# Row minima of the masked attention scores: one masked pass and one reduction for a unit instead of one fused instruction for a block

## The chip, the cores and the metric

The kernel runs on one core of one Trainium2 chip. The metric is device time in microseconds (us) of one execution. Three runs of the kernel before gave a median of 922.48 us (921.83 to 923.4). Engines: PE is TensorE (matmuls), DVE VectorE, ACT ScalarE, POOL GpSimd, SP SyncE, which issues the DMAs.

## The reference

Sparse attention over 4 batches and 8 heads of 576 positions (head width 64), followed by two dense feed-forward layers, all in float32. Only the attention part matters here:

```
scores = (1/sqrt(64)) * q @ k.T
scores = where(mask, scores, -1e9)     # heads 0-3: the last 32 positions; heads 4-7: every 32nd position
scores = scores - max(scores, row)
attn = exp(scores)
attn = attn / (sum(attn, row) + 1e-9)
x = attn @ v                           # then x -> mish layer -> gated SiLU layer
```

## The kernel before

The feed-forward layers are matmuls with every float32 operand split into a high and a low part, so that three matmuls stand for one product (`mm3`, line 83). They fill nearly the whole span. The attention is worked off beside the first of these matmuls.

**Units.** The attention is cut into 48 units, numbered from 0. A unit belongs to one batch and one pair of heads (`hp`) and holds three or four blocks. In the local pairs (`hp` 0 and 1) a block is 128 rows of scores by 96 keys and a unit has three blocks; in the strided pairs (`hp` 2 and 3) a block is 108 rows by 64 keys, and three units of a pair have 4, 4 and 3 blocks. So there are 24 local units, 16 strided units of four blocks and 8 of three. The order is local pairs first, then strided ones, three units to a pair (in the last batch the strided ones come first).

**Steps of a unit.** `at_qk`: PE writes the scores of all blocks to one PSUM bank `sc` (line 303), and DVE forms the negated, scaled, masked scores `pt` in SBUF and their row minima in `sm[:, 0]` (line 315). `at_exp`: ACT takes exp(min - pt) block by block, in place, and leaves the row sums in `sm[:, 1]` (line 330). `at_norm`: DVE adds 1e-9 to the sums (line 343) and takes reciprocals (line 344), and POOL multiplies `pt` by them (line 345). `at_tr` transposes on PE (line 361), `at_copy` copies the result to SBUF on DVE (line 373), `at_pv` multiplies with v on PE (line 386), `at_hi` and `at_lo` split the output on ACT (line 74) and DVE (line 79).

**What sets the order.** The program order on each engine is written out by hand. A step `k` of the list `DENSE` runs `at_qk` and `at_exp` of unit k, `at_norm` of unit k-1, `at_tr` and `at_copy` of unit k-3, `at_pv` and `at_hi` of unit k-4, `at_lo` of unit k-5. The first 29 steps are run so. Between two of them stand a few idle matmuls (`spin`), one product of the first layer, and one of the four operations with which DVE rebuilds a weight tile from its stored bits (lines 207, 210, 213, 216). When a weight tile is rebuilt, ACT makes its high part (line 74) and POOL its low part (line 79). The other 19 units follow in the list `LOOSE`, in three pieces per unit, beside a denser stream of matmuls. Three times ACT applies Mish to a chunk of the first layer (line 494), which takes a change of its function table before and after.

**What the change touches.** `at_qk` from line 312 and `at_norm` at line 343, and one constant, the value at masked places in `_layout`.

Of the kernel before, what the change touches and what calls it, by code (L numbers as in the profile page):

```python
# [12 lines left out]
ALU = mybir.AluOpType  # L13
# [41 lines left out]
def local_strided_attention__mish_moe__swiglu_kernel(  # L55
# [10 lines left out]
    nc = tc.nc  # L66
# [20 lines left out]
    masks = [cst[:, 0:96], cst[:, 96:192], cst[:, 192:256]]  # L87
# [16 lines left out]
    for i in range(NP):  # L104
        for kind in "gv":
            k = "gv".index(kind)
# [160 lines left out]
    for i, (b, hp) in enumerate(pairs):  # L267
        nb, st_ = (NLB, 3) if hp < 2 else (NSB, 4)
# [21 lines left out]
    def blk(hp, j):  # L290

        if hp < 2:
            return LB, LK, j * LB, masks[0 if j == 0 else 1]
        return SW, 64, SR[j] * NJ, masks[2]

    def at_qk(u):
        i, b, hp, js = units[u]
        t = qk_t[i]
        sc = ps.tile([128, 512], F32, tag="sc", name="sc", bufs=2)
        w = blk(hp, js[0])[1]  # L300
        for jj, j in enumerate(js):
            nq, nk, j0, m = blk(hp, j)
            nc.tensor.matmul(  # L303
                sc[:2 * nq, jj * w:(jj + 1) * w],
                lhsT=t[:, 2 * j * nq:2 * (j + 1) * nq],
                rhs=t[:, QW + j0:QW + j0 + nk],
                start=True,
                stop=True,
            )
        pt = sb.tile([128, 4 * 96], F32, tag="pt", name="pt", bufs=6)[:2 * nq, :len(js) * w]  # L310
        pt = pt.rearrange("p (j k) -> p j k", k=w)
        sm = small.tile([128, 2, 4], F32, tag="sm", name="sm", bufs=5)[:2 * nq]
        for jj, j in enumerate(js):
            m = blk(hp, j)[3]
            nc.vector.tensor_tensor_reduce(  # L315
                pt[:, jj],
                sc[:2 * nq, jj * w:(jj + 1) * w],
                m[:2 * nq],
                -0.125,
                3.0e38,  # L320
                ALU.add,
                ALU.min,
                accum_out=sm[:, 0, jj:jj + 1],
            )
        st[u] = (pt, sm)

    def at_exp(u):
# [11 lines left out]
    def at_norm(u):  # L339
        pt, sm = st[u]  # L340
        n, nb, w = pt.shape
        r = sm[:, 1, :nb]
        nc.vector.tensor_scalar_add(r, r, 1e-9)
        nc.vector.reciprocal(r, r)  # L344
        nc.gpsimd.tensor_tensor(out=pt, in0=pt, in1=r.unsqueeze(2).to_broadcast([n, nb, w]), op=ALU.mult)  # L345

# [77 lines left out]
    def at_v(u):  # L424
        if u % 2:
# [5 lines left out]
        [  # L431
            (at_load, 0),
            (at_qk, 0),
            (at_tr, 3),
            (at_pv, 4),
            (at_v, 4),
            (at_exp, 0),
            (at_norm, 1),
            (at_lo, 5),
            (at_copy, 3),  # L440
            (at_hi, 4),
        ]
    ]
    LOOSE = [
        [(at_load, 0), (at_norm, 1), (at_lo, 5), (at_qk, 0), (at_exp, 0)],
        [(at_tr, 3), (at_copy, 3)],
        [(at_pv, 4), (at_hi, 4), (at_v, 4)],
# [174 lines left out]
    fv, fs, f4 = {}, {}, [None]  # L622
# [261 lines left out]
def _layout(q, k, v, moe_w_in, moe_w_out, moe2_w_gate, moe2_w_val, moe2_w_out):  # L884
    import numpy as np

    f4 = np.float32

    def heads_t(a):
        return a.reshape(B, 4, 2, S, D).transpose(0, 1, 2, 4, 3).reshape(B, 4, 128, S)  # L890

    def residue_major(a):
        return a.reshape(B, 2, 128, NJ, STR).transpose(0, 1, 2, 4, 3).reshape(B, 2, 128, S)

    qt, kt = heads_t(q), heads_t(k)
    qt[:, 2:], kt[:, 2:] = residue_major(qt[:, 2:]), residue_major(kt[:, 2:])
    qk = np.zeros((B, 4, 128, QW + KW), f4)
    for hp in range(4):
        n, first = (LB, range(0, S, LB)) if hp < 2 else (SW, [r * NJ for r in SR])
        for j, q0 in enumerate(first):  # L900
            for h in range(2):
                p = slice(64 * h, 64 * h + 64)
                qk[:, hp, p, (2 * j + h) * n:(2 * j + h + 1) * n] = qt[:, hp, p, q0:q0 + n]
    qk[:, :2, :, QW + STR:] = kt[:, :2]
    qk[:, 2:, :, QW:QW + S] = kt[:, 2:]

    vp = v.reshape(B, 4, 2, S, D).transpose(0, 1, 3, 2, 4).reshape(B, 4, S, 128)
    v_loc = np.zeros((B, 2, 3, LK, 3, 128), f4)
    for j in range(NLB):
        lo = j * LB - STR  # L910
        a = max(0, -lo)
        v_loc[:, :, j // 3, a:, j % 3] = vp[:, :2, lo + a:lo + LK]
    vr = vp[:, 2:].reshape(B, 2, NJ, STR, 128).transpose(0, 1, 3, 2, 4).reshape(B, 2, S, 128)
    v_str = np.zeros((B, 2, 3, 128, 4, 128), f4)
    for j in range(NSB):
        k0, p0 = SR[j] * NJ, 64 * (j % 2)
        m = min(64, S - k0)
        v_str[:, :, j // 4, p0:p0 + m, j % 4] = vr[:, :, k0:k0 + m]

    def bits(w):  # L920
        return w.view(np.int64) if w.dtype == np.float64 else w

    def col_tiles(w):
        w = bits(w)
        n = w.shape[1] // 128
        return w.reshape(4, 128, n, 128).transpose(2, 1, 0, 3).reshape(n, 128, 512)

    w1 = np.stack([col_tiles(moe_w_in), bits(moe_w_out).reshape(FF1 // 128, 128, DM)], axis=2)
    w2 = np.stack([col_tiles(moe2_w_gate), col_tiles(moe2_w_val), bits(moe2_w_out).reshape(FF2 // 128, 128, DM)], axis=2)

    p, c = np.arange(128)[:, None], np.arange(LK)[None, :]
    rel = p % LB - (c - STR)
    local = (rel >= 0) & (rel < STR)

    w, i = np.arange(64)[None, :], p % SW
    strided = (i // NJ == w // NJ) & (w % NJ <= i % NJ)
    keep = np.concatenate([local & (c >= STR), local, strided], axis=1)
    consts = np.concatenate([np.where(keep, f4(0), f4(-8e9)), np.eye(128, dtype=f4)], axis=1)
    return {
        "qk": qk.reshape(B * 4, 128, QW + KW),  # L940
        "v_loc": v_loc.reshape(B * 2, 3, LK, 3, 128),
        "v_str": v_str.reshape(B * 2, 3, 128, 4, 128),
        "w1": w1,
        "w2": w2,
        "consts": consts,
    }
# [21 lines left out]
```

## Time and profile before

| | before |
|---|---|
| median of three runs | 922.48 us |
| profiled execution: time, span | 920.13 us, 918.3 us |
| granted TensorE clock | 0.999 (of 2.4 GHz) |
| busy PE, DVE, ACT, POOL | 900.5, 602.0, 381.8, 162.9 us |
| chain that ended last | PE 87%, DVE 5%, DMA 3%, ACT 2% |

The profiled execution is one run, and its own time stands 1.8 us above its span. Busy shares are means over stages of different kind: from about 165 us on, PE is busy almost without a gap, and the attention is over; before that the engines take turns at being late. So the first 165 us are to be read stretch by stretch. In a list of instructions by time, the first column is the start and the second the duration; where an instruction starts before the one in front of it has ended, the two overlap, and the time that the engine spends on one is the distance from start to start.

### The profile page before, as it was taken

The numbers are of one execution on the slowest core, as the hardware profiler recorded it, in microseconds if no ns is written. First come the engines' busy times: TensorE is split into PE (matmuls) and PEld (weight loads), VectorE is DVE, ScalarE is ACT, GpSimd is POOL, SyncE is SP. The second block draws the span as 40 slices with busy tenths as digits, with TensorE's granted clock in tenths as the row PEclk, the third lists the DMA queues.
The fourth block names the chain that finished last, engine by engine and source line by source line (L and its number), as shares of the span: only waits on it lengthen the run. The fifth ranks groups of instructions, "written<-read, shape, count | busy, mean of one in ns | idle before, by whom it ended". The sixth has DMA issues, their size and how long they took to land.

```text
span 918.3 us, 13830 instructions
## 1 busy us (share of the span) xinstructions
PE 900.5 (98%) x4983; PEld 751.6 (82%) x4987; DVE 602.0 (66%) x1382; ACT 381.8 (42%) x951; POOL 162.9 (18%) x153
## 2 busy tenths in 40 slices
PE   8988999999999999999999999999999999999998
PEld 5776886888888888888889888888888888888886
DVE  5997576778876797769556788848435644334434
ACT  5667654525443444434243554423324423322230
POOL 3445141400000000000022322203113221112211
PEclk9999999999999999999999999999999999999999
DMA  8875431324643254524106887675532545552322
GB/s 290 282 254 179 146 116 50 115 92 165 212 174 115 95 198 176 172 70 161 69 1 262 290 330 303 259 287 191 186 121 109 207 153 191 186 203 92 138 92 91
DMA packets 48499, 156.70 MB, mean 171 GB/s; under 512 B 5296, under 2 KB 11824, under 8 KB 48432
## 3 DMA queue, kind: packets, MB, share of 16 engines
q1 hardware_dynamic: 48432, 155.83, 47.9%
q8 instruction: 39, 0.64, 0.3%
q14 instruction: 28, 0.23, 0.1%
HBM read 119.64 MB, written 36.18 MB: 170 GB/s over the span
## 4 chain that ended last, share of the span: by engine, by line
PE 87%; DVE 5%; DMA 3%; ACT 2%; issue 1%; POOL 1%; SPq 1%; POOLq 0%; ACTq 0%; DVEq 0%
PE h L83 20%; PE y L83 18%; PE o L83 16%; PE cXv L83 7%; PE cXg L83 7%; PE c L83 4%; PE cZg L83 3%; PE cZv L83 3%; PE sc L303 2%; PE cYv L83 2%; PE cYg L83 2%; PE xp L386 2%; DMA rawl<-in_w_dram 1%; PE tp L361 1%; DMA raw<-in_w_dram 1%
## 5 line engine op out<-in xcount | busy, mean ns | idle before, releaser
L83 PE MATMUL y<-g,w 128*128 128x512 f32 (+1 forms) x960 | 206.4, 371 | 0.0
L83 PE MATMUL h<-xh,w 128*128 128x512 f32 (+1 forms) x640 | 196.2, 376 | 0.4 <-ACT xh L74 0.4
L83 PEld LDWEIGHTS y<-g,w 128*128 128x128 f32 x960 | 165.7, 189 | 29.0
L83 PE MATMUL o<-wr,fs 128*128 128x512 f32 x648 | 149.6, 389 | 0.0
L83 PEld LDWEIGHTS o<-wr,fs 128*128 128x128 f32 x648 | 121.3, 188 | 24.9
L83 PEld LDWEIGHTS h<-xh,w 128*128 128x128 f32 x640 | 116.4, 189 | 20.9 <-ACT xh L74 0.6
L83 PE MATMUL h<-xl,w 128*128 128x512 f32 (+1 forms) x320 | 118.1, 369 | 0.0
L79 POOL TENSOR_TENSOR fs<-k,fs 128x512 fp32r<-128x512 f32 x36 | 48.5, 1348 | 268.2 <-ACT fs L74 216.1
L490 ACT ACTIVATE u<-h 128x512 f32<-128x512 f32 (+1 forms) x68 | 37.2, 547 | 140.6 <-PE h L83 140.6
L719 DVE TENSOR_TENSOR acc<-acc,o 128x512 f32<-128x512 f32 x90 | 61.4, 685 | 48.6 <-PE o L83 48.5
L330 ACT ACTIVATE pt<-pt,sm 108x64 f32<-108x64 f32 (+1 forms) x160 | 55.8, 350 | 48.4 <-DVE sm L315 48.2
L83 PEld LDWEIGHTS h<-xl,w 128*128 128x128 f32 x320 | 60.5, 189 | 8.5 <-DVE xl L79 0.3
L79 POOL TENSOR_TENSOR B<-acc,B 128x512 fp32r<-128x512 f32 x6 | 8.3, 1391 | 297.0 <-ACT B L74 297.0
L74 ACT CAST fs<-k 128x512 fp32r<-128x512 f32 x36 | 22.4, 622 | 87.9 <-DVE k L674 37.6
L660 DVE TENSOR_TENSOR k<-cZg,k 128x512 f32<-128x512 f32 x12 | 8.3, 691 | 73.2 <-PE cZg L83 73.2
L83 PE MATMUL cXv<-T,wr 128*128 128x512 f32 x216 | 54.9, 390 | 0.7 <-ACT k L657 0.7
L83 PE MATMUL cXg<-T,wr 128*128 128x512 f32 x216 | 54.8, 389 | 0.0
L79 DVE TENSOR_TENSOR g<-u,g 128x512 fp32r<-128x512 f32 (+1 forms) x68 | 43.1, 654 | 13.9 <-ACT g L74 13.9
L74 ACT CAST ws<-wt 128x512 fp32r<-128x512 f32 x60 | 37.0, 616 | 35.6 <-DVE wt L216 31.7
L74 ACT CAST g<-u 128x512 fp32r<-128x512 f32 (+1 forms) x80 | 44.5, 574 | 15.5 <-PE y L83 15.4
L345 POOL TENSOR_TENSOR pt<-pt,sm 128x288 f32<-128x288 f32 (+2 forms) x48 | 35.4, 738 | 83.9 <-DVE sm L344 61.9
L83 PEld LDWEIGHTS cXv<-T,wr 128*128 128x128 f32 x216 | 40.5, 188 | 9.5 <-ACT k L657 1.1
(102 smaller groups left out, 1440.0 us busy)
## 6 DMA issues: line engine op xcount, KB each, us to landing
raw<-in_w_dram SPq DMA_DIRECT2D x54, 512.0 KB, 3.8
qk<-in_qk_dram SPq DMA_DIRECT2D x16, 898.0 KB, 6.9
wr<-wd_g_S SPq DMA_DIRECT2D x24, 512.0 KB, 7.4
wr<-wd_v_S SPq DMA_DIRECT2D x24, 512.0 KB, 8.0
wr<-wd_p SPq DMA_DIRECT2D x24, 512.0 KB, 4.7
wr<-wd_g_W SPq DMA_DIRECT2D x18, 512.0 KB, 6.5
wr<-wd_v_W SPq DMA_DIRECT2D x18, 512.0 KB, 7.1
rawl<-in_w_dram SPq DMA_DIRECT2D x14, 512.0 KB, 5.6
```

The costliest lines, as they stand in the source:

```text
L74: nc.scalar.copy(hi, src)
L79: eng.tensor_tensor(out=lo, in0=src, in1=hi.bitcast(F32), op=ALU.subtract)
L83: nc.tensor.matmul(o, lhsT=lhs, rhs=rhs, start=first and i == 0, stop=last and i == 2, skip_group_check=more)
L303: nc.tensor.matmul(sc[:2 * nq, jj * w:(jj + 1) * w], lhsT=t[:, 2 * j * nq:2 * (j + 1) * nq], rhs=t[:, QW + j0:QW + j0 + nk], start=True, s ...
L330: nc.scalar.activation(out=pt[:, jj], in_=pt[:, jj], func=AF.Exp, scale=-1.0, bias=sm[:, 0, jj:jj + 1], accum_out=sm[:, 1, jj:jj + 1],)
L345: nc.gpsimd.tensor_tensor(out=pt, in0=pt, in1=r.unsqueeze(2).to_broadcast([n, nb, w]), op=ALU.mult)
L361: nc.tensor.transpose(tp[:k, o:o + n], src, ident[:n, :n])
L386: nc.tensor.matmul(xp[64 * h:64 * h + 64, o:o + nq - skip], lhsT=vt[:nk, jj, 64 * h:64 * h + 64], rhs=ts[:nk, c0 + h * nq + skip:c0 + (h + ...
L490: nc.scalar.activation(out=u, in_=p, func=AF.Mish)
L660: nc.vector.tensor_tensor(out=t, in0=p, in1=t, op=ALU.add)
L719: nc.vector.tensor_tensor(out=acc[c][:, t], in0=acc[c][:, t], in1=o, op=ALU.add)
```

## The change

Line 315 was one instruction for each block: it read the scores and the mask, wrote (score + mask) times -0.125 and kept the running minimum in an accumulator, which a second instruction then read out to `sm`. After the change one SCALAR_TENSOR_TENSOR writes score times -0.125 plus mask for all blocks of the unit, with the mask repeated over the blocks by its access pattern, and one TENSOR_REDUCE reads `pt` back and writes the minima of all blocks. Only the first of the three units of a local pair has two masks, and there two SCALAR_TENSOR_TENSOR stand in front of the TENSOR_REDUCE. The masked places hold 1e9 instead of -8e9, since the mask is now added after the scaling. At line 343 the 1e-9 was added by a TENSOR_SCALAR; now a SCALAR_TENSOR_TENSOR computes max(r + 1e-9, r), with `r` as both of its inputs.

```
-        for jj, j in enumerate(js):
-            m = blk(hp, j)[3]
-            nc.vector.tensor_tensor_reduce(
-                pt[:, jj], sc[:2 * nq, jj * w:(jj + 1) * w], m[:2 * nq], -0.125, 3.0e38,
-                ALU.add, ALU.min, accum_out=sm[:, 0, jj:jj + 1])
+        at = 0
+        for m, nb in ((masks[0], 1), (masks[1], len(js) - 1)) if js[0] == 0 and hp < 2 else ((blk(hp, js[0])[3], len(js)),):
+            nc.vector.scalar_tensor_tensor(
+                pt[:, at:at + nb],
+                sc[:2 * nq, at * w:(at + nb) * w].rearrange("p (j k) -> p j k", k=w), -0.125,
+                m[:2 * nq].unsqueeze(1).to_broadcast([2 * nq, nb, w]), op0=ALU.mult, op1=ALU.add)
+            at += nb
+        nc.vector.tensor_reduce(sm[:, 0, :at], pt, axis=mybir.AxisListType.X, op=ALU.min)
...
-        nc.vector.tensor_scalar_add(r, r, 1e-9)
+        nc.vector.scalar_tensor_tensor(r, r, 1e-9, r, op0=ALU.add, op1=ALU.max)
...
-    consts = np.concatenate([np.where(keep, f4(0), f4(-8e9)), np.eye(128, dtype=f4)], axis=1)
+    consts = np.concatenate([np.where(keep, f4(0), f4(1e9)), np.eye(128, dtype=f4)], axis=1)
```

On DVE, a strided unit of four blocks in the dense steps (unit 19). `ISA pt,sm<-sc,cst` is the fused instruction of a block, `ISA sm` the one that reads its accumulator out. Before:

```order
L488 COPY u<-h 128x512
L315 ISA pt,sm<-sc,cst 108x64
L315 ISA sm 108x1
L315 ISA pt,sm<-sc,cst 108x64
L315 ISA sm 108x1
L315 ISA pt,sm<-sc,cst 108x64
L315 ISA sm 108x1
L315 ISA pt,sm<-sc,cst 108x64
L315 ISA sm 108x1
L343 TENSOR_SCALAR sm<-sm 108x4
L344 RECIPROCAL sm<-sm 108x4
```

The same place with the change:

```order
L488 COPY u<-h 128x512
L315 SCALAR_TENSOR_TENSOR pt<-sc,cst 108x256
L324 TENSOR_REDUCE sm<-pt 108x4
L343 SCALAR_TENSOR_TENSOR sm<-sm 108x4
L344 RECIPROCAL sm<-sm 108x4
```

Eight instructions became two, and each of the four blocks' scores is now passed over twice, once from PSUM and once from SBUF. Nothing else changed its place.

On DVE, the first unit of a local pair (unit 15), with the change; before, three fused instructions of 128x96 and three accumulator reads stood between the same neighbours:

```order
L207 TENSOR_SCALAR wtmp<-raw 128x512
L315 SCALAR_TENSOR_TENSOR pt<-sc,cst 128x96
L315 SCALAR_TENSOR_TENSOR pt<-sc,cst 128x192
L324 TENSOR_REDUCE sm<-pt 128x3
L343 SCALAR_TENSOR_TENSOR sm<-sm 128x3
L344 RECIPROCAL sm<-sm 128x3
```

Here two passes with different masks stand ahead of the reduction, which reads what both have written.

On ACT, the exponentials of two early local units, with the semaphores that each waits for (a difference: - before, + with the change):

```order
-L330 ACTIVATE pt,sm<-pt,sm 128x96 [waits DVE_49] x6
+L330 ACTIVATE pt,sm<-pt,sm 128x96 [waits DVE_49]
+L330 ACTIVATE pt,sm<-pt,sm 128x96 x2
+L330 ACTIVATE pt,sm<-pt,sm 128x96 [waits DVE_49]
+L330 ACTIVATE pt,sm<-pt,sm 128x96 x2
 L74 CAST xh_68<-xp 128x192 [waits PE_49]
```

Before, each exponential waited for DVE's minimum of its own block; now the first one of a unit waits for the reduction over all blocks, and the others wait for nothing more.

## Rows read from the trace of the kernel before

**Rows 1.** Busy time by stretch: window, length, busy (instructions), clock, DMA share, GB/s

```profile
12.19:41.18 28.99, 26.37 (x290) 21.05 (x292) 26.21 (x147) 20.60 (x105) 12.80 (x14) 1.00 0.80 275
41.18:72.67 31.49, 27.98 (x297) 22.76 (x295) 30.98 (x148) 20.73 (x101) 14.87 (x15) 1.00 0.73 248
72.67:87.75 15.08, 12.44 (x98) 9.44 (x96) 9.57 (x49) 12.80 (x41) 7.64 (x8) 1.00 0.69 222
87.75:144.78 57.03, 57.03 (x511) 45.80 (x511) 35.88 (x212) 34.07 (x158) 17.71 (x23) 1.00 0.36 116
144.78:163.48 18.70, 16.67 (x127) 12.56 (x126) 12.87 (x34) 11.25 (x26) 3.31 (x4) 1.00 0.16 49
```

**Rows 2.** Chain of waits: start, length, what

```profile
72.06 0.34 DVE wtmp L207
...
72.67 1.18 ACT pt L330 x6
...
146.20 1.19 ACT pt L330 x6
...
147.41 1.28 ACT L494
```

**Rows 3.** DVE by time, a local unit: start, duration, instruction

```profile
34.52 0.24 DVE L315 CUSTOM_DVE_ANT_0 pt<-sc,cst 128x96 f32<-128x96 f32 x1
34.69 0.08 DVE L315 DVE_READ_ACCUMULATOR2_ANT sm<- 128x1 f32 x1
34.69 0.24 DVE L315 CUSTOM_DVE_ANT_0 pt<-sc,cst 128x96 f32<-128x96 f32 x1
...
35.05 0.16 DVE L343 TENSOR_SCALAR sm<-sm 108x3 f32<-108x3 f32 x1
35.24 0.18 DVE L344 RECIPROCAL sm<-sm 108x3 f32<-108x3 f32 x1
...
35.95 0.68 DVE L213 SCALAR_TENSOR_TENSOR wtmp<-raw,wtmp 128x512 int32<-128x512 int32 x1
36.56 0.24 DVE L315 CUSTOM_DVE_ANT_0 pt<-sc,cst 128x96 f32<-128x96 f32 x1
```

**Rows 4.** DVE by time, a strided unit of four blocks, first row to next line

```profile
61.87 0.21 DVE L315 CUSTOM_DVE_ANT_0 pt<-sc,cst 108x64 f32<-108x64 f32 x1
...
62.44 0.16 DVE L343 TENSOR_SCALAR sm<-sm 108x4 f32<-108x4 f32 x1
```

**Rows 5.** DVE groups by shape: count, busy us, mean ns, idle before

```profile
L315 DVE CUSTOM_DVE_ANT_0 pt<-sc,cst 128x96 f32<-128x96 f32 x72 | 14.6, 251 | 9.7 <-PE sc L303 9.1 <-PE tp L361 0.5
L315 DVE CUSTOM_DVE_ANT_0 pt<-sc,cst 108x64 f32<-108x64 f32 x88 | 14.5, 217 | 4.4 <-PE sc L303 3.5 <-PE tp L361 0.7
L79 DVE TENSOR_TENSOR xl<-xp,xh 128x192 fp32r<-128x192 f32 x22 | 7.3, 331 | 0.2 <-ACT xh L74 0.2
L534 DVE TENSOR_TENSOR acc<-acc,y 128x256 f32<-128x256 f32 x12 | 4.3, 415 | 4.0 <-PE y L83 4.0
```

**Rows 6.** DVE by time, idle before, and what ended it

```profile
29.11 0.23 DVE L315 CUSTOM_DVE_ANT_0 pt<-sc,cst 108x64 f32<-108x64 f32 x1 [0.68 <-PE tp L361]
...
31.89 0.23 DVE L315 CUSTOM_DVE_ANT_0 pt<-sc,cst 108x64 f32<-108x64 f32 x1 [0.75 <-PE sc L303]
```

**Rows 7.** DVE by time, the last unit

```profile
145.91 0.25 DVE L315 CUSTOM_DVE_ANT_0 pt<-sc,cst 128x96 f32<-128x96 f32 x1
```

**Rows 8.** POOL by time

```profile
37.63 0.67 POOL L345 TENSOR_TENSOR pt<-pt,sm 128x288 f32<-128x288 f32 x1 [1.54 <-DVE sm L344]
...
41.27 1.28 POOL L79 TENSOR_TENSOR w<-wtmp,w 128x512 fp32r<-128x512 f32 x1 [0.67 <-ACT w L74]
```

**Rows 9.** DVE by time, beside these two

```profile
37.92 0.92 DVE L216 SCALAR_TENSOR_TENSOR wtmp<-w,wtmp 128x512 f32<-128x512 f32 x1
38.84 0.26 DVE L315 CUSTOM_DVE_ANT_0 pt<-sc,cst 128x96 f32<-128x96 f32 x1
...
41.72 0.85 DVE L343 TENSOR_SCALAR sm<-sm 128x3 f32<-128x3 f32 x1
```

**Rows 10.** Line 343 alone in the dense steps: window, length, DVE busy, clock, DMA

```profile
12.19:72.67 60.48, 7.29 (x23) 1.00 0.77 261
```

**Rows 11.** Line 343 in that stretch: count, duration min/median/max ns

```profile
L343 DVE TENSOR_SCALAR sm<-sm x23: 155/165/847, 12.7 to 70.3; 128x3 f32<-128x3 f32 x11, 108x4 f32<-108x4 f32 x8, 108x3 f32<-108x3 f32 x4
```

More of the change, by code (lines that the diff above doesn't have):

```diff
@@ L312, in at_qk @@
         sm = small.tile([128, 2, 4], F32, tag="sm", name="sm", bufs=5)[:2 * nq]
-        for jj, j in enumerate(js):
-            m = blk(hp, j)[3]
-            nc.vector.tensor_tensor_reduce(
-                pt[:, jj],
-                sc[:2 * nq, jj * w:(jj + 1) * w],
-                m[:2 * nq],
+        at = 0
+        for m, nb in ((masks[0], 1), (masks[1], len(js) - 1)) if js[0] == 0 and hp < 2 else ((blk(hp, js[0])[3], len(js)),):
+            nc.vector.scalar_tensor_tensor(
+                pt[:, at:at + nb],
+                sc[:2 * nq, at * w:(at + nb) * w].rearrange("p (j k) -> p j k", k=w),
                 -0.125,
[L320 to L323, printed above, removed]
-            )
+                m[:2 * nq].unsqueeze(1).to_broadcast([2 * nq, nb, w]),
+                op0=ALU.mult,
+                op1=ALU.add,
+            )
+            at += nb
+        nc.vector.tensor_reduce(sm[:, 0, :at], pt, axis=mybir.AxisListType.X, op=ALU.min)
         st[u] = (pt, sm)
```

## The prediction

> **What bounds the kernel now.** I read the busy time by stretch first. From 87.75 to 144.78 us PE is busy for all of 57.03 us while DVE works 35.88 [rows 1]: what the change adds to DVE there lies beside matmuls. From 41.18 to 72.67 us it is the other way: DVE is busy 30.98 of 31.49 us and PE 27.98, so DVE is the bound. From 12.19 to 41.18 us DVE is busy 26.21 of 28.99 and PE 26.37: the two are level, and DVE has 2.78 us in hand. From 72.67 to 87.75 us neither is full; there ACT, busy 12.80 of 15.08, leads. The chain of waits says how the bound passes on: at 72.67 us from DVE to the exponentials of unit 26, behind which ACT goes on with weights and Mish, and at 146.20 us to the exponentials of unit 47, the last, behind which the table for Mish is loaded [rows 2]. From 163 us on the attention is over, and a delay won or lost before reaches the end in full.
>
> Then DVE by time, for what one unit costs. A fused instruction on 128x96 lasts 0.24 us, but the next one starts 0.17 to 0.18 us after it, and the accumulator read of 0.08 us runs inside the overlap: three blocks take 35.05 - 34.52 = 0.53 us [rows 3]. Four strided blocks take 62.44 - 61.87 = 0.57 us [rows 4], 0.143 each, so three take 0.43. The sums of durations (3 x (0.25 + 0.08) = 1.0) would say nearly twice that.
>
> **The change on DVE.** The trace has no masked pass of a whole unit and no TENSOR_REDUCE. The nearest rows for the pass are TENSOR_TENSOR with an input in PSUM: 331 ns at 192 elements, 415 at 256 [rows 5], 1.3 ns an element between them; the fused instructions go 217 to 251 ns for 32 elements, 1.06 each. I take 0.45 us at 288. A following instruction that does not need the result starts some 0.07 us before the end: the 512-element pass of 0.68 us is followed after 36.56 - 35.95 = 0.61 [rows 3]. One that does need it starts after the end: line 344 reads what line 343 wrote, and starts 0.19 us after a start of 0.16 us duration, 0.03 us behind its end. The reduction reads what the pass wrote, so it waits so.
>
> For the reduction itself I take the same duration as a pass of as many elements. Below, it can't beat one element at the slope of 1.06 ns (0.31 us at 288, 0.14 less); above, it may go at half that rate (0.31 us more). It is nearest in kind to the other one-pass rows, so the middle value stands and both ends go into the range.
>
> A unit then costs DVE:
> - local, one mask: 0.45 + 0.03 + (0.45 - 0.07) = 0.86, was 0.53: +0.32 to +0.33, taken as 0.32;
> - local, two masks: 0.25 - 0.07, then 0.33 + 0.03 + 0.38 = 0.92: +0.38;
> - strided, four blocks: 0.415 + 0.03 + 0.345 = 0.79, was 0.57: +0.22;
> - strided, three: 0.33 + 0.03 + 0.26 = 0.62, was 0.43: +0.19.
>
> Over all 48 units (16, 8, 16, 8 of these) that is 13.2 us of DVE time. What of it is on the path:
> - Units 3 to 14 (12.19 to 41.18 us): 0.38 + 0.64 + 0.63 + 0.63 + 0.38 + 0.64 = 3.3 us (unit 3; 4 and 5; 6 to 8; 9 to 11; 12; 13 and 14). DVE's 2.78 us of idling there ended on PE's scores and transposes, 0.68 and 0.75 us the largest [rows 6]; PE in turn waits for DVE's copies, so only part of the slack can be used. All of it would leave 0.5, none of it 3.3; I take the middle, 1.9.
> - Units 15 to 25 (to 72.3 us), DVE full: 0.38 + 0.64 + 1.26 + 0.70 = 3.0 us, in full (unit 15; 16 and 17; 18 to 23; 24 and 25).
> - Unit 26: ACT takes over. Before, the first exponential started as soon as the first block's minimum was there, 146.20 - 145.91 = 0.29 us after the first fused instruction of a local unit [rows 2, 7]. Now it waits for both passes, 0.45 + 0.03 + 0.45 = 0.93 us: +0.6. The same for unit 47 at 146 us: +0.6. Between the two this delay lies beside PE.
> - In six of the dense steps line 343 waits for POOL (next part). POOL's work there is released by ACT, which is 0.6 us later than before, while DVE is later by two units' worth, 0.4 to 0.64: some 0.07 a step, 0.4 in all.
>
> Units 27 to 46 otherwise cost nothing: ACT's Mish covers 27 and 28, PE the rest. If PE's cover were gone for a third of the 18 units from 29 to 46, it would be about 6 x 0.25 = 1.5 us.
>
> **The 1e-9.** The two-source instruction on 3 or 4 elements is as short as the one it replaces. What line 343 pays is waiting: 23 in the dense steps take 7.29 us [rows 10] with a median of 165 ns [rows 11], so 7.29 - 3.80 = 3.5 us are waits, in six of them. The one at 41.72 us ran 0.85 us, to 42.57; POOL's operation beside it ended at 42.55 [rows 8, 9]. So it got its inputs about 0.15 us before POOL ended. Does a two-source instruction escape that? A row answers: line 216, whose two tensors lie in SBUF, started at 37.92 us inside POOL's operation of 37.63 to 38.30 and took 0.92 us instead of 0.68. It too ran as if started 0.14 us before POOL ended. So the new form waits the same, and I count 0.
>
> **Sum.** 1.9 + 3.0 + 0.6 + 0.6 + 0.4 = +6.5 us. The profiled execution took 920.13 us, so 926.6; the median of the runs shown is 2.35 us above it, and on that scale the forecast is 929.0 us.
>
> **Rivals.**
> 1. *Faster, since fewer instructions.* If each DVE instruction paid its full duration, the sums of durations would count: a local unit 1.0 before and 0.90 after, 1.03 with two masks; a strided one of four 4 x (0.217 + 0.08) = 1.19 and 0.83; of three 0.89 and 0.66. Units 3 to 26 would win 8 x 0.10 - 4 x 0.03 + 8 x 0.36 + 4 x 0.23 = 4.5 us and lose 1.2 by the two later exponentials: -3.3, 919.2 us. It decides if the rows after show the pass and the reduction together shorter than 0.53 us, or if line 315 stood further apart than its rows say. Against it stand the starts at 34.52, 34.69 and 35.05 us [rows 3]. 8%. The Trainium skill, "VectorE: DVE Perf Modes", speaks for this rival ("Rules for kernel authors": minimise the number of operations; "The DRAIN you can't avoid": the next operation does not start until the pipe is empty). By its errata table (58 or 120 cycles plus one per element at 0.96 GHz) a strided unit of four would fall from 1.01 to 0.72 us, an estimate. The trace disagrees in the count: starts stand 0.143 us apart, less than that fixed part and 64 elements together (0.19).
> 2. *The two-source form does not wait for POOL.* Then 3.5 us come back: 925.5. For it: line 343's shortness, and that a tiny instruction may get in between two reads. Against it: line 216. 12%.
> 3. *The waits swallow the addition.* If POOL's operations keep their time, the six waits of about 0.6 us absorb the extra of the units ahead of them, about 0.5 each, and the 0.4 goes: 929.0 - 3.4 = 925.6. Against it: POOL's operand comes from ACT, behind exponentials that start later. 12%.
> 4. *The reduction goes at half rate.* +0.31, +0.27 and +0.20 us on the 24 units from 3 to 26: 12 x 0.31 + 8 x 0.27 + 4 x 0.20 = 6.7, and the last unit 0.3: 936.0. 10%.
>
> **Numbers.** The forecast has 58%; its own range is 926.5 to 932. The range of 924.5 to 934.5 us takes in rivals 2 and 3 and leaves out 1 and most of 4. Within 0.2% (1.8 us, about what a measurement of this kernel can tell) stands 924.3 at the upper end: faster 0.06, nearly all of rival 1; same 0.06, from the rest of it and the lower edges of 2 and 3; slower 0.88.
>
> **What would show it.** The TENSOR_REDUCE should start 0.03 us behind the pass and the pair hold DVE for 0.79 us in a strided unit of four. DVE should be full from 15 to about 78 us, unit 26's exponentials should start near 72.67 + 1.9 + 3.0 + 0.6 + 0.4 = 78.6 us, and PE's gapless stretch near 93.7 us instead of 87.75. Line 343 should still have waits of 0.6 us. The stretch after 163 us should last as long as before. The prediction is wrong if unit 26 comes at less than 2 us later, if line 343's waits are gone, or if PE idles in the stretch that was gapless.

## The result and the profile after

The median with the change is 929.64 us (928.95 to 931.04, 4 runs); the kernel before took 922.15 us (919.86 to 923.4) beside it. The ratio is 1.0087 [1.0072, 1.0101]: slower, by 7.5 us from median to median, where 6.5 were forecast and 929.0 us named. One thing has to be known to read the times below: they scatter with TensorE's granted clock. Runs of the kernel before go from 919.06 us at a mean clock of 1.000 to 924.58 us at 0.994, and runs with the change have 0.996 or 0.994.

| | before | after |
|---|---|---|
| profiled execution: time, span | 920.13, 918.3 us | 929.7, 927.9 us |
| mean granted clock | 0.999 | 0.996 |
| busy PE, DVE, ACT, POOL | 900.5, 602.0, 381.8, 162.9 us | 905.2, 612.1, 381.3, 163.1 us |
| DVE instructions | 1382 | 1166 |

DVE has 216 instructions less and is busy 10 us longer. Where that reaches the end is read by stretch, as in [rows 1] (window, length, then busy PE, PEld, DVE, ACT, POOL, clock, DMA share, GB/s):

```profile
12.19:44.00 31.81, 28.90 (x310) 22.47 (x309) 30.08 (x97) 21.38 (x106) 13.77 (x15) 1.00 0.77 271
44.00:78.00 34.00, 27.84 (x287) 22.73 (x285) 33.10 (x96) 20.17 (x100) 14.15 (x15) 1.00 0.69 221
94.00:95.00 1.00, 1.00 (x7) 0.85 (x4) 0.70 (x2) 0.67 (x4) 1.00 (x2) 0.71 0.16 65
95.00:96.00 1.00, 1.00 (x7) 0.87 (x6) 0.55 (x1) 1.00 (x7) 0.28 (x1) 0.50 0.00 0
96.00:97.00 1.00, 1.00 (x5) 0.94 (x5) 0.86 (x5) 0.49 (x2) 0.41 (x1) 0.50 0.00 0
97.00:98.00 1.00, 1.00 (x5) 0.65 (x4) 0.63 (x2) 0.24 (x1) 1.00 (x2) 0.58 0.00 0
...
94.00:150.00 56.00, 55.54 (x477) 44.25 (x474) 36.15 (x123) 32.01 (x151) 16.65 (x23) 0.97 0.35 110
...
164.00:166.00 2.00, 2.00 (x16) 1.60 (x13) 1.47 (x3) 0.32 (x1) 0.00 (x0) 0.50 0.38 39
```

From 44 to 78 us DVE is the bound: 33.10 busy of 34.00, PE 27.84. Then two things stand here that [rows 1] do not have: PE is no longer busy for the whole of the stretch from 94 to 150 us, and the clock is at its lower level (0.50 is 1.2 GHz) around 96 and 165 us.

DVE by time (start, duration, instruction): where unit 3 starts, a two-mask unit (unit 15), a strided unit of four blocks and unit 26; they answer to [rows 3, 4 and 9]:

```profile
12.41 0.51 DVE L315 SCALAR_TENSOR_TENSOR pt<-sc,cst 128x96 f32<-128x96 f32 x2
...
42.60 0.51 DVE L315 SCALAR_TENSOR_TENSOR pt<-sc,cst 128x96 f32<-128x96 f32 x2
43.14 0.45 DVE L324 TENSOR_REDUCE sm<-pt 128x3 f32<-128x288 f32 x1
43.51 1.25 DVE L343 SCALAR_TENSOR_TENSOR sm<-sm 128x3 f32<-128x3 f32 x1
...
55.62 0.41 DVE L315 SCALAR_TENSOR_TENSOR pt<-sc,cst 108x256 f32<-108x256 f32 x1
56.06 0.42 DVE L324 TENSOR_REDUCE sm<-pt 108x4 f32<-108x256 f32 x1
56.40 0.81 DVE L343 SCALAR_TENSOR_TENSOR sm<-sm 108x4 f32<-108x4 f32 x1
...
76.97 0.44 DVE L315 SCALAR_TENSOR_TENSOR pt<-sc,cst 128x288 f32<-128x288 f32 x1
77.44 0.45 DVE L324 TENSOR_REDUCE sm<-pt 128x3 f32<-128x288 f32 x1
77.81 0.15 DVE L343 SCALAR_TENSOR_TENSOR sm<-sm 128x3 f32<-128x3 f32 x1
```

A unit's cost is the distance from its first start to line 343's: 0.91, 0.78 and 0.84 us for the last three. The reduction starts 0.03 us behind the pass's end each time (43.11 and 43.14, 56.03 and 56.06, 77.41 and 77.44), and line 343 starts inside the reduction. Two instances of line 343 here take 1.25 and 0.81 us instead of 0.15. POOL by time, beside the first of them:

```profile
43.45 1.29 POOL L79 TENSOR_TENSOR w<-wtmp,w 128x512 fp32r<-128x512 f32 x1 [1.05 <-ACT w L74]
```

POOL ends at 44.74, line 343 at 44.76: the two-source form waits for POOL as the old one did in [rows 8, 9].

The same two places before, DVE by time: the first instruction of unit 15 and of unit 26.

```profile
41.18 0.26 DVE L315 CUSTOM_DVE_ANT_0 pt<-sc,cst 128x96 f32<-128x96 f32 x1 [0.31 <-PE tp L361]
...
72.32 0.24 DVE L315 CUSTOM_DVE_ANT_0 pt<-sc,cst 128x96 f32<-128x96 f32 x1
```

So unit 15 starts 42.60 - 41.18 = 1.42 us later and unit 26 76.97 - 72.32 = 4.65 us later. Of the 1.42, 12.41 - 12.19 = 0.22 us are there at unit 3 already. In front of unit 3 DVE stands idle in both traces until a DMA has landed (2.48 us before, 1.85 with the change), and this start scatters: in the traces of kernels with the old scores in these units it lies anywhere from 12.04 us (e11) to 12.94 (e9). So the 0.22 can't be put down to the scores. The chain of waits after says how that goes on (start, length, what):

```profile
77.04 0.38 DVE pt L315
77.44 0.45 DVE sm L324
...
77.99 1.19 ACT pt L330 x6
...
79.99 1.28 ACT L494
```

The exponentials of unit 26 start at 77.99 us, against 72.67 in [rows 2]: +5.32. PE by time, its waits of over 0.1 us from 87 us to the end of the attention, with the idle time and what ended it in brackets, with the change:

```profile
93.08 0.51 PE L361 MATMUL tp<-cst,pt 128*96 128x128 f32 x3 [1.77 <-DVE sm L343]
...
119.17 0.38 PE L361 MATMUL tp<-cst,pt 108*128 108x108 f32 x2 [0.46 <-DVE ts L373]
...
162.14 0.50 PE L361 MATMUL tp<-cst,pt 128*96 128x128 f32 x3 [2.75 <-DVE ts L373]
```

And before:

```profile
87.75 0.50 PE L361 MATMUL tp<-cst,pt 128*96 128x128 f32 x3 [1.75 <-DVE sm L343]
...
153.65 0.50 PE L361 MATMUL tp<-cst,pt 128*96 128x128 f32 x3 [2.03 <-DVE ts L373]
```

PE comes out of the wait behind the first Mish 93.08 - 87.75 = 5.33 us later: of the 5.32 nothing is lost or gained in between. The wait of 0.46 us at 119.17 has no counterpart before. The last one, behind the last Mish, has become 0.72 us longer.

### The profile page after: what moved, and what is told of

Its sections match the earlier page's. It is cut to its first block, busy times and chain, and to the rows that moved or that the text cites. A ratio compares the mean times of both kernels' runs of the same rounds, so it can differ in the third digit from the quotient of the medians.

```text
span 927.9 us, 13646 instructions
## 1 busy us (share of the span) xinstructions
PE 905.2 (98%) x4987; PEld 753.9 (81%) x4987; DVE 612.1 (66%) x1166; ACT 381.3 (41%) x951; POOL 163.1 (18%) x153
## 4 chain that ended last, share of the span: by engine, by line
PE 85%; DVE 7%; DMA 3%; ACT 3%; issue 1%; SPq 1%; POOL 0%; POOLq 0%; ACTq 0%; DVEq 0%
PE h L83 20%; PE y L83 18%; PE o L83 16%; PE cXv L83 7%; PE cXg L83 7%; PE c L83 4%; PE cZv L83 3%; PE cZg L83 3%; PE cYv L83 2%; PE cYg L83 2%; PE xp L386 2%; PE sc L303 1%; DMA rawl<-in_w_dram 1%; PE tp L361 1%; DVE sm L324 1%
```

## The experiments

Each was timed beside runs of the kernel before on the same chip; the ratio is against those.

**The two edits apart.** e1 has line 343 in its new form and the old scores; e2 the new scores and the old line 343.

```
e1 (against before)
-        nc.vector.tensor_scalar_add(r, r, 1e-9)
+        nc.vector.scalar_tensor_tensor(r, r, 1e-9, r, op0=ALU.add, op1=ALU.max)
e2 (against after): the same two lines, the other way round
```

> Only the 1e-9 is added by the two-source instruction; the scores are worked as before. Theory (a two-source instruction waits for POOL as the one-source one did): no change, within 0.5 us of before, and line 343 still takes about 7.3 us for its 23 in the dense steps. Rival (it escapes the wait): line 343 takes 23 x 0.16 = 3.7 us there, and the kernel is up to 3.5 us faster than before.

> Only the scores are masked and reduced in the new way; 1e-9 is added by the one-source instruction of before. Theory: the whole slowdown, 7 to 8 us over before. Rival (the add has a share of its own): 1 us or more away from the 7.5 us of the whole change.

e1: 920.94 us (919.08 to 924.5), ratio 1.0001 [0.999, 1.0012]. e2: 929.53 us (927.22 to 931.46), ratio 1.0093 [1.0079, 1.0107]. The scores are the whole of it. Line 343 alone in the trace of e1, window as in [rows 10]:

```profile
12.19:72.67 60.48, 7.14 (x23) 0.98 0.77 260
```

7.14 us against 7.29: the waits for POOL are all there. Rival 2 falls.

**Early and late units apart.** e3 has the new scores in units 29 to 47, e4 in units 0 to 28, the others are as before. In both, and in e9 and e10, the mask keeps its -8e9 and is subtracted instead of added.

```
+        if u >= 29:     # e3;   e4: if u < 29:
+            ... pass and reduction
+        else:
             ... fused instruction of a block
```

> The new scores in units 29 to 47 alone (19 of 48), the old ones in 0 to 28; the new ones subtract a mask of -8e9 instead of adding 1e9. Theory: PE covers these units but for the last one, whose exponentials start 0.6 us later, and 0.5 us of one new wait of PE: +1 us, and up to +2.5 if TensorE's clock falls behind PE's wait at 150 to 154 us as in the changed kernel. Rival (every unit pays alike): 19/48 of 7.5 = +3.0 us.

> The new scores in units 0 to 28 alone, the old ones in 29 to 47. Theory: PE's gapless stretch starts 5.3 us later than before (93.1 us instead of 87.75); the kernel is 5.3 us slower, or 7 where the clock falls at 94 us as in the changed kernel. Rival (every unit pays alike): 29/48 of 7.5 = +4.5 us, and the stretch before 93 us shows no more than that.

e4: 928.22 us (924.52 to 929.22), ratio 1.0074 [1.0059, 1.0089]. e3: 923.99 us (922.74 to 925.66), ratio 1.0032 [1.002, 1.0044]. The medians add up to more than the whole, 6.8 + 2.55 us, and e3's 2.55 does not tell its two answers (up to 2.5, and 3.0) apart. Both hold a share of the clock: it was below 0.996 in three of e4's six runs and one of e3's five, and in none of the seventeen of the kernel before. At like clocks they come out lower: the one run of e4 at a mean clock of 1.000 took 924.52 us, three of before at that clock 919.06 to 919.94, so the early units cost some 4.9. In that trace PE comes out of the wait behind the first Mish at 93.17 us, where the theory had 93.1 and units that pay alike would give 87.75 + 4.5 = 92.3:

```profile
93.17 0.50 PE L375 MATMUL tp<-cst,pt 128*96 128x128 f32 x3 [1.76 <-DVE sm L357]
```

Three runs of e3 at 0.996 have a median of 923.99, four of before 922.26: some 1.7 for the late units, under the 3.0 of units that pay alike, but more than the prediction's 0.6.

**The clock.** Is the rest the clock? A few idle matmuls on a zero tile, issued where PE would wait behind the two Mish passes, keep PE busy there. e5 puts them into the changed kernel, e6 into the one before.

```
+HOLD = {30: 8, 49: 12}      # e5;   e6: {30: 8, 49: 9}
+    def hold(n):
+        wp = ps.tile([128, 512], F32, tag="sc", name="wh", bufs=2)
+        for _ in range(n):
+            nc.tensor.matmul(wp, lhsT=wz[:, :128], rhs=wz, start=True, stop=True)
...
+        if p == 1 and k in HOLD:
+            hold(HOLD[k])
```

> The changed kernel with idle matmuls (8 and 12, on zeros, into a bank of the scores that is free) put into PE's order where it waits at 91.3 to 93.1 us and at 159.4 to 162.1 us. Theory (1 to 2 us of the slowdown are TensorE's clock, granted at half behind these two waits): the mean granted clock comes to 0.999 or 1.0, and the time to 926 us, 3.5 us under the changed kernel and 5 us over before. Rival (the clock's fall has no share, or comes elsewhere): no change, 929.6 us.

> The kernel before with the same idle matmuls (8 and 9) in the same two waits of PE. Theory: its runs of 919 us at clock 1.0 and of 922 us at 0.996 come together at 919 to 919.8 us, 1.5 to 2 us under before's median. Rival: no change.

e5: 926.12 us (925.92 to 927.42), ratio 1.0048 [1.0035, 1.006], 3.5 us under the change alone. e6: 919.88 us (918.94 to 920.72), ratio 0.9977 [0.9968, 0.9986]. Both now have mean clocks of 0.998 to 1.000, most of them 1.000. The stretch behind the first wait in e5 (columns as above), and PE by time in that wait:

```profile
94.00:96.00 2.00, 1.98 (x20) 1.29 (x19) 1.93 (x7) 0.34 (x2) 1.59 (x3) 1.00 0.59 219
96.00:98.00 2.00, 2.00 (x17) 1.74 (x16) 1.20 (x5) 1.82 (x10) 0.94 (x2) 1.00 0.04 18
```

```profile
92.48 1.90 PE L455 MATMUL wh<-wz 128*128 128x512 bf16 x7
```

The clock that was 0.50 in the change's trace at 95 to 97 us is 1.00. Between the two kernels with idle matmuls stand 926.12 - 919.88 = 6.2 us: what the change costs with the clock nearly held. The other 7.5 - 6.2 = 1.3 us of the medians I put down to the clock. The intervals of the ratios are as wide as that, so its size is an estimate; that the clock has a share is seen in the 0.50 above and in e6, 2.0 us under the kernel before.

**The reduction by itself.** e7 does the TENSOR_REDUCE twice in every unit, which says what one more of it costs where DVE is full.

```
         nc.vector.tensor_reduce(sm[:, 0, :at], pt, axis=mybir.AxisListType.X, op=ALU.min)
+        nc.vector.tensor_reduce(sm[:, 0, :at], pt, axis=mybir.AxisListType.X, op=ALU.min)
```

> The changed kernel with the reduction of every unit done twice, the second writing the same minima over the first. Theory (DVE's time in units 3 to 26 is on the path in full): each second reduction costs 0.48, 0.45 or 0.38 us (its duration and 0.03 us of waiting), 5.4 us in units 3 to 14, 5.0 in 15 to 25, 0.5 at unit 26 and 0.5 at unit 47: +11 us over the changed kernel. Rival (waits for POOL and PE's slack swallow half of what DVE is given): +5.5 us.

945.64 us (940.32 to 947.24), ratio 1.0238 [1.0214, 1.0262]: 16 us over the change, more than either answer. Its least disturbed run, at a mean clock of 0.998, took 940.32, 10.7 over the change's median; but the change's own runs are at 0.996 and 0.994, and the one run of e2 at 0.998 took 927.22, 13.1 less. The others of e7 have 0.980 to 0.989. In the profiled one (0.98) PE is busy for 21.69 of the 28 us from 12 to 40, with the change for 25.17, and behind them the clock is low in the dense steps themselves:

```profile
40.00:50.00 10.00, 8.87 (x62) 7.34 (x59) 8.06 (x28) 4.70 (x25) 1.84 (x3) 0.57 0.70 231
```

So e7 says that DVE's time in the dense steps comes to the end in full or nearly so (13.1 us between two single runs at like clock, where 11 were forecast), and not more exactly than that: most of its runs hold a share of the clock.

**No addition at all.** e8 is the kernel before without line 343 (the 1e-9 is left out; the row sums are at least 1, where float32 does not hold it). The line's waits and its own time together were 3.5 + 3.8 us of DVE.

```
-        nc.vector.tensor_scalar_add(r, r, 1e-9)
```

> The kernel before without the addition of 1e-9 at line 343 (a row's largest exponential is 1, so the sum is at least 1 and float32 doesn't hold the 1e-9). Theory: 23 times 0.19 us and 3.5 us of waits for POOL leave DVE in the dense steps, and at least those of the stretch where DVE is full come to the end: 11 x 0.19 + 2.4 = 4.5 us faster than before, up to 6. Rival (the wait for POOL passes to the next instruction that reads two tensors from SBUF, or PE takes over as the bound at once): 1 to 2 us faster.

917.33 us (916.85 to 919.65), ratio 0.9953 [0.994, 0.9967]. That is 4.6 us under the kernel before, where 4.5 were forecast, and PE leaves the wait behind the first Mish at 83.36 us instead of 87.75. The reciprocal could have inherited the wait for POOL and did not. All of its instances in the dense steps (count, duration min/median/max), and one of them by time with POOL's operation around it:

```profile
L343 DVE RECIPROCAL sm<-sm x25: 162/170/177, 12.7 to 71.1; 128x3 f32<-128x3 f32 x13, 108x4 f32<-108x4 f32 x8, 108x3 f32<-108x3 f32 x4
```

```profile
39.81 0.17 DVE L343 RECIPROCAL sm<-sm 128x3 f32<-128x3 f32 x1
```

```profile
39.36 1.29 POOL L79 TENSOR_TENSOR w<-wtmp,w 128x512 fp32r<-128x512 f32 x1 [0.87 <-ACT w L74]
```

**Units 27 to 46.** The step "units 27 to 46 otherwise cost nothing" looked wrong. e9 is e6 with the new scores in these units alone.

```
+        if 27 <= u <= 46:
+            ... pass and reduction
```

> Pass and reduction in units 27 to 46 alone, the fused form in the others, the 1e-9 as before, and the idle matmuls of e6 (8 and 9) in PE's two waits, so that the clock scatters less. e6, the same without the new units, took 919.88 us. The prediction's own step (units 27 to 46 cost nothing, Mish and PE cover them): 919.9, within 0.3. Rival, from the wait of 0.46 us that PE has at 119.17 us in the trace with the change: these units do cost, as the copies that PE waits for are late there: 920.4 to 921.0, and a wait of PE for a copy to SBUF between 109 and 121 us.

920.24 us (919.89 to 921.36), ratio 0.9983 [0.9973, 0.9993]; e6 had 0.9977. By the time alone (0.36 us over e6) the two answers can't be told apart. The trace tells them apart. The stretch from 87 to 150 us, first e6, then e9:

```profile
87.00:150.00 63.00, 62.98 (x559) 49.87 (x558) 39.68 (x228) 37.66 (x168) 19.93 (x26) 1.00 0.35 116
```

```profile
87.00:150.00 63.00, 62.34 (x545) 48.85 (x544) 42.47 (x146) 35.33 (x165) 20.14 (x27) 1.00 0.36 114
```

PE is busy 0.64 us less, and the largest of its new waits is this one (PE by time, e9), for a copy by DVE as at 119.17 us above:

```profile
112.91 0.38 PE L376 MATMUL tp<-cst,pt 108*128 108x108 f32 x2 [0.32 <-DVE ts L388]
```

The other traces agree: each one with the new scores in units 29 to 46 has a wait of PE for that copy between 112 and 135 us (e2 0.45, e3 0.33, e5 0.47, e10 0.33 us), and none with the old ones there has (before, e1, e4, e6, e8, e11).

**Units 26 and 47.** e10 keeps the fused form in these two, where ACT waits for the first block, and the old line 343.

```
+        if u not in (26, 47):
             ... pass and reduction
+        else:
+            ... fused instruction of a block
```

> Pass and reduction everywhere but in units 26 and 47, which keep the fused form; the 1e-9 by the old instruction. Theory: those two units alone let ACT start its exponentials after the first block, so they give back 0.6 us each: unit 26's first exponential near 77.4 us instead of 77.99, the time 928.3 to 928.6 against 929.6 of the whole change. Rival: unit 26's delay is DVE's, not the first block's, and the gain is below 0.2 us at 26, or none: 929.3 to 929.6.

927.89 us (927.2 to 928.37), ratio 1.0069 [1.0056, 1.0082]: 1.75 us under the change and a little below the forecast, at a mean clock of 0.996 in four of five runs as there. The intervals of the two ratios overlap, so the trace has to show it. Unit 26 starts at 78.33 us on DVE in the profiled run (the clock had fallen to 0.95 from 12 to 44 us, which moved everything behind), so its place on the clock says nothing; its exponentials start 0.34 us behind it, against 77.99 - 76.97 = 1.02 with the change. The last unit in the chain of waits of e10:

```profile
153.15 0.69 DVE u L502
...
154.37 0.17 DVE pt L329
...
154.58 1.18 ACT pt L344 x6
...
162.02 0.50 PE tp L375 x3
```

The same copy of Mish's input in the chain before, and in the chain with the change:

```profile
144.78 0.69 DVE u L488
```

```profile
152.54 0.69 DVE u L488
```

From the copy of Mish's input to PE's transposes it is, in e10, 162.02 - 153.15 = 8.87 us, as before the change (153.65 - 144.78 = 8.87); with the change it is 162.14 - 152.54 = 9.60.

**Both gains.** e11 is e8 with the idle matmuls of e6.

```
-        nc.vector.tensor_scalar_add(r, r, 1e-9)
+        if p == 1 and k in HOLD:      # HOLD = {30: 8, 49: 9}, hold() as above
+            hold(HOLD[k])
```

> The kernel before without the addition of 1e-9 (left out: the row sums are 1 at least, where float32 does not hold it) and with the idle matmuls of e6 (8 and 9) in PE's two waits. If the two gains are of different kinds (POOL's waits on DVE, TensorE's clock) they add: e8 took 917.33 and the idle matmuls gave 2.3 us in the kernel before, so 915.2 to 916.0. Rival: with the addition gone PE's waits end at another time and the number of idle matmuls no longer fits, so they fill nothing or delay the scores: 916.8 to 918.

915.99 us (914.97 to 916.71), ratio 0.994 [0.9927, 0.9953], at clocks of 0.999 and 1.000. The median reaches the upper end of the forecast, 1.3 us under e8, and the intervals of the two ratios overlap. It is faster than both kernels, for reasons that have nothing to do with the scores.

## Why the prediction was right, and where it was off

Each step, forecast and measured (us):

| step | forecast | measured |
|---|---|---|
| unit: local, two masks, strided of four | 0.86, 0.92, 0.79 | 0.84, 0.91, 0.78 |
| unit 3's start, behind a DMA | not in it | 0.22 |
| units 3 to 14 | 1.9 | 1.42 - 0.22 = 1.20 |
| units 15 to 25, with the drift of POOL's waits | 3.0 + 0.4 | 4.65 - 1.42 = 3.23 |
| unit 26's later exponentials | 0.6 | 5.32 - 4.65 = 0.67 |
| units 27 to 46 | 0 | 0.46 (after), 0.64 (e9) of waits on PE |
| unit 47's later exponentials | 0.6 | 9.60 - 8.87 = 0.73 |
| the 1e-9 | 0 | ratio 1.0001 (e1) |
| sum, without unit 3's start | 6.5 | 1.20 + 3.23 + 0.67 + 0.46 + 0.73 = 6.3; 6.2 by e5 and e6 |
| TensorE's clock | not in it | some 1.3 of the medians |

That the sums stand 0.2 us apart is in part luck: the forecast had 0.7 us too much in units 3 to 14 and 0.2 in 15 to 25, and 0.07, 0.46 and 0.13 too little in unit 26, in 27 to 46 and in 47. Unit 26's exponentials, forecast near 78.6 us, came at 77.99, and PE's stretch from 93.7 at 93.08; what was lost later made it up. That 929.0 us stand so near the 929.64 measured is too: the clock's share was not in the forecast.

*What was right.* The way the durations were joined: a fused block costs the distance between starts, and the reduction, which needs all of the pass, costs the pass's full length first. The groups of DVE by shape show that a reduction lasts as long as a pass of equal size, the middle value:

```profile
L324 DVE TENSOR_REDUCE sm<-pt 128x3 f32<-128x288 f32 x24 | 10.9, 453 | 0.8
L315 DVE SCALAR_TENSOR_TENSOR pt<-sc,cst 128x288 f32<-128x288 f32 x16 | 7.1, 445 | 0.3 <-PE sc L303 0.3
L324 DVE TENSOR_REDUCE sm<-pt 108x4 f32<-108x256 f32 x16 | 6.7, 420 | 0.6
L315 DVE SCALAR_TENSOR_TENSOR pt<-sc,cst 108x256 f32<-108x256 f32 x16 | 6.6, 415 | 1.0 <-PE sc L303 0.6 <-issue 0.2
```

That ends rival 4 (half rate) and rival 1: the pair takes 0.84 us, not under 0.53. The page "VectorE: DVE Perf Modes" of the Trainium skill ("Rules for kernel authors") advises a minimum of operations; 216 fewer of them cost 6.2 us here, because a unit's two instructions take longer than its many did: a strided unit of four went from 0.57 to 0.78 us while its instructions went from eight to two. The same page of the Trainium skill ("The DRAIN you can't avoid") says that the next operation does not start until the pipe is empty, and goes on that one which is not held starts earlier; rival 1 in the prediction has the first half alone. The trace shows both: the reduction, which reads the pass's result, starts 0.03 us behind its end, and line 343, which does not read the reduction's, starts at 77.81, 0.08 us before the reduction ends.

*POOL's waits.* With the change line 343 takes 7.53 us in 24 instances from 12.19 to 78 us. At its median of 152 ns that leaves 7.53 - 24 x 0.152 = 3.9 us of waits, against 3.5 before: the drift of 0.4 came, but as five longer waits (0.47 to 1.25 us) in place of six. Rival 3, waits that swallow the addition, falls by the same number.

*What was too high.* In units 3 to 14 it was the 3.3 us of added time, not the share of the slack. The stretch of these units with the change (columns as in [rows 1]):

```profile
12.41:42.60 30.19, 27.28 (x294) 21.25 (x293) 28.50 (x93) 19.76 (x102) 13.22 (x14) 1.00 0.77 270
```

DVE's idle time fell from 28.99 - 26.21 = 2.78 us to 30.19 - 28.50 = 1.69, and 12 x 0.03 = 0.36 of the latter are the reductions' own waits for the pass. So some 1.4 us of slack went, the half that was assumed, and 1.20 + 1.4 = 2.6 us were added. Two of the reasons: line 343 took 2.82 us in these units instead of 3.08, and unit 6 had cost 0.97 us before (18.52 to 19.49) instead of 0.57.

*What was too low.* Two steps. The first had been named in the prediction as a sign of its being wrong: PE idles in the stretch that was gapless. "Units 27 to 46 otherwise cost nothing ... PE the rest" rested on PE being busy for all of 57.03 us [rows 1]. A PE that is always busy does not say by how much its inputs are early. The copy of a transposed tile stands on DVE behind the next unit's pass and reduction, and it came late once here and twice in e9. The chain of waits with the change shows the place:

```profile
117.85 0.43 DVE pt L315
118.29 0.02 issue
118.31 0.42 DVE sm L324
118.73 0.30 DVE ts L373
119.03 0.14 issue
119.17 0.38 PE tp L361 x2
```

And "the stretch after 163 us should last as long as before" took the clock as given: from the transposes at 162.14 us to the end it is 927.9 - 162.14 = 765.76 us, before 918.3 - 153.65 = 764.65, and 2 us at 0.50 (164 to 166 us) do the work of 1: that is most of the 1.1 us. In the profiled runs the span grew by 9.6 us, of which 6.5 are the steps above with unit 3's start; most of the other 3.1 is the clock: 0.29 + 0.50 + 0.50 + 0.42 = 1.7 us from 94 to 98, and these 1.1. The medians hold only some 1.3 of it, since the kernel before loses time to the clock too, in most of its runs; its profiled run (0.999) was one of the better ones. The forecast added the 2.35 us between that run and the median, and so held the share that the kernel before has already, but not the change in it.

*What stays open.* Why the clock falls behind a wait in one run and not in the next. The first wait is 1.75 us long before and 1.77 after; before, the clock stayed at 1.00 behind it in the profiled run, and in the profiled run of e1, whose wait is of 1.76 us, it fell:

```profile
90.00:92.00 2.00, 2.00 (x9) 1.68 (x9) 0.70 (x3) 1.38 (x6) 0.81 (x1) 0.50 0.05 22
```

In e8 the wait is of 1.80 us, and the clock is 1.00 from 83 to 90 us. Nor does it fall behind these waits alone: it is 0.95 from 12 to 44 us in the profiled runs of e5 and e10, and 0.96 from 12 to 40 us in that of e1, which has the old scores. So 1.3 us is what these runs had on average, not a property of the change that could be worked out from one trace.

## What to carry to other kernels

Fewer instructions are not less time: read the distance between starts, since work that overlaps its neighbours costs less than its duration, and an instruction that reads its forerunner's whole output gets no overlap at all (here it started 0.03 us behind the end). Where several blocks are merged into one step, ask who was waiting for the first block; that wait ends with the last one now. And an engine that is busy all the time shows no slack of the engines that feed it: count the time between a tile's readiness and its use before costing a delay there at nothing.

## What had not been expected

- TensorE's clock fell to 0.50 behind a wait of 1.77 us on PE, and differs from run to run of the same kernel; 17 idle matmuls in two waits took 2.0 us off the kernel before (921.9 to 919.88, ratio 0.9977 [0.9968, 0.9986]).
- An addition of 1e-9 to three or four numbers a row cost 4.6 us (921.9 to 917.33, ratio 0.9953 [0.994, 0.9967]); 3.5 of the 7.3 us that it held DVE were waits for POOL. RECIPROCAL on the same numbers does not wait (177 ns at most, seven of 25 inside POOL's operations), and none of the 48 reductions is longer than 454 ns, though eight of them lie inside POOL's operations. The Trainium skill, "SBUF — State Buffer" ("Who interferes with whom"), says that `tensor_scalar` can contend with GpSimd and `tensor_reduce` cannot; the trace agrees in both (0.85 us for a TENSOR_SCALAR [rows 9], and the 454 ns).
- With a second reduction a unit, four of e7's five runs have a mean clock below 0.99, and no run of any other kernel here has; in the trace it is 0.57 from 40 to 50 us. That PE's longer waits for DVE bring this about is argued, not shown.
